# Exponentials of a chunk's last rows: a step on the PSUM read in place of a step on the SBUF write

## The chip, the cores and the metric

The kernel runs on one core of a Trainium2 chip. The metric is the device time of one execution in microseconds. Before the change it is 180.93 us, the median of 3 runs (180.81 to 181.0). A difference is read against runs of the kernel before on the same chip.

## What is computed

A gated linear attention over 4 batches, 8 heads, 768 steps and a head size of 48, and behind it one mixer block with weights over tokens (768 to 256 and back) and over channels (384 to 1536 and back). All matrices come in and go out as float32.

```python
f = 1.0 / (1.0 + np.exp(-f_logit))
for t in range(S):
    state = f[:, :, t, :, None] * state + np.einsum('bhd,bhe->bhde', k[:, :, t], v[:, :, t])
    y[:, :, t] = np.einsum('bhd,bhde->bhe', q[:, :, t], state)
x = np.ascontiguousarray(y.transpose(0, 2, 1, 3)).reshape(B, S, H * D)
xt = x.transpose(0, 2, 1)
u = x + (np.maximum(xt @ w_tok1, 0.0) @ w_tok2).transpose(0, 2, 1)
out = u + np.maximum(u @ w_ch1, 0.0) @ w_ch2
```

## The kernel before

**Tiling.** Each batch's 768 steps are cut into 6 chunks of 128, with the step on the partitions. Inside a chunk the recurrence is replaced by matmuls: the gates' logarithms are summed over the steps of the chunk by a matmul with a triangle of ones (L554, L555), and ScalarE takes from that bank in PSUM the exponential with both signs (`G` and `Gi`, L565 and L567). VectorE multiplies q by `G` and k by `Gi` in one operation (L586), TensorE turns the products (L603; for the last batch a DMA does that), the scores are made (L504), masked on VectorE into `AmT` (L640) and multiplied with v (L678). From chunk to chunk goes a `state`: L652 adds the chunk's own part, L654 multiplies by `glast`, the decay over the whole chunk, which is the exponential of the sum at the chunk's last step, and copies of it (`state_bd`, through the copy helper at L459 to L463) feed L671.

**Where the changed line stands.** `glast` must lie with the head's channel on the partitions: partition (par, d) and column hp, for head 2 hp + par and channel d. The sums have the step on the partitions. So for batches 1 to 3 and every chunk but the last (15 times) L574 takes the exponentials of the sums' last 32 rows (partitions 96 to 127, since an instruction begins at such a boundary here) into `ends`, and a small DMA (`across`, L580, on SyncE's queue) carries row 127 of `ends` to the 128 partitions of `glast`. `ends` is laid out as (par, d, hp) with room for 64 channels, so that row 127, read from front to back, gives each partition of `glast` its 4 floats side by side. The sums in PSUM are laid out as (hp, par, d). Batch 0 makes `glast` with matmuls of its own (L570). There are 4 buffers of `ends` and `glast`.

**The mixer.** L708 and L724 are the two token matmuls, L740 on VectorE adds the residual, L459 casts to `u_bf`, L765 turns it, L783 is the first channel matmul with its ReLU on ScalarE (L468) or VectorE (L470), L802 the second, with the residual on VectorE (L808) and the output's DMA (L812).

**What sets the order.** Every operation is entered with `add` into a plan, with the engines that may do it, a rank, a model of its cost and the bank of PSUM that it uses. The plan lays all operations out by this model, helped by a table of ranks and delays by operation number (`SHIFTS`), and the instructions are then issued in that order on each engine. The order is fixed when the kernel is built; each engine takes its instructions in turn and waits where one isn't ready. The model's cost of L574 is that of 384 elements from PSUM, `el = ("el", DM, True, 1)`, whatever the steps of its operands. The kernel uses 8 banks of PSUM; a bank comes free for the next matmul when its last reader is done, and L574 is one of the readers of the sums' bank.

Of the kernel before, what the change touches and what calls it, by code (L numbers as in the profile page):

```python
# [12 lines left out]
AF = mybir.ActivationFunctionType  # L13
# [103 lines left out]
class Plan:  # L117
# [11 lines left out]
    def add(self, engines, rank, fn, need=(), make=(), bank=None, kind=("fix", 100, 100), tail_of=None, room=1):  # L129


        engines = (engines,) if isinstance(engines, str) else engines
        op = Op(engines, rank, fn, need, make, bank, kind)
        for key in need:
            if key in self.maker:
                op.before.add(self.maker[key])
        for key in make:
            if key in self.maker:
                op.before.add(self.maker[key])
            op.before.update(self.users.get(key, ()))  # L140
        for key in need:
            self.users.setdefault(key, []).append(op)
        for key in make:
            self.maker[key], self.users[key] = op, []
        if bank is not None:
            key = bank
            if key in self.maker:
                op.before.add(self.maker[key])
            if engines == (PE,):
                self.maker[key] = op  # L150
        if kind[0] == "load":
            line = self.loads[engines[0]]
            if line:
                op.behind = line[-1]
            line.append(op)
        op.room = room
        if tail_of is not None:
            while tail_of is not None:
                tail_of.before |= op.before - {tail_of}
                tail_of.tail = tail_of.tail or op  # L160
                tail_of = next((x for x in self.ops if x.tail is tail_of), None)
        self.ops.append(op)
        return op
# [137 lines left out]
def kernel(  # L301
# [13 lines left out]
    B, H, S, D = q.shape  # L315
# [11 lines left out]
    def st(shape, dtype, tag):  # L327
        return sb.tile(shape, dtype, tag=tag, name=tag)
# [26 lines left out]
    ends = [st([128, 2, 64, HP], FP32, f"ends{i}") for i in range(4)]  # L355
# [131 lines left out]
    def attention(b, cs, due):  # L487

        nb = b % NB
        heads = [sums_and_turns(b, c, due(b, c) - (3.0 if b >= TURNED else 0.0)) for c in cs]  # L490
        p_d, live = Bank(), [c for c in cs if c < NCH - 1]
        need = [("qkT", c % 4, p) for c in cs for p in range(2)]
# [37 lines left out]
    def sums_and_turns(b, c, r):  # L530
        i, i4, nb, g4 = c % 2, c % 4, b % NB, (b * NCH + c) % 4
# [29 lines left out]
        def sview():  # L561
            return banks[p_s.at][:, 0:DM].rearrange("t (h d) -> t h d", d=D)
# [6 lines left out]
        if not last and b < 1:  # L569
            add(ACT, r + 1.0, lambda: nc.scalar.activation(  # L570
                glast[g4], banks[p_s.at][:, DM:DM + HP], AF.Exp, bias=0.0, scale=-1.0),
                make=[("glast", g4)], bank=p_s, kind=("el", 4, True, 1))
        elif not last:
            add(ACT, r, lambda: nc.scalar.activation(  # L574
                ends[g4][96:128, :, 0:D].rearrange("t par d hp -> t hp par d"),
                sview()[96:128].rearrange("t (hp par) d -> t hp par d", par=2), AF.Exp, bias=0.0, scale=-1.0),
                make=[("ends", g4)], bank=p_s, kind=el)

            def across():
                nc.sync.dma_start(out=glast[g4], in_=ends[g4][127:128].rearrange("o par d hp -> o (par d) hp"))  # L580

            add(SP, r, across, need=[("ends", g4)], make=[("glast", g4)],
                kind=("fix", 600, (5200, 5200, 3400)[b - 1], 300))
# [299 lines left out]
```

## Time and profile before

| | |
|---|---|
| median of 3 runs | 180.93 us |
| the profiled execution | 180.95 us, of which the span of its instructions is 179.1 us |
| granted TensorE clock | 1.00 |
| busy: TensorE, VectorE, ScalarE, GpSimd | 166.3, 128.1, 125.8, 100.7 us |
| L574, all 15 | 12.7 us of ScalarE, first at 39.3, last at 129.2 us |
| L580, the DMA behind it | 15 times 2 KB, 4.3 us from issue to landing (median) |

PE is TensorE (PEld its weight loads), DVE is VectorE, ACT is ScalarE, POOL is GpSimd and SP is SyncE. A row of a group gives line, engine, operation, what is written from what is read, shapes and count, then the group's busy time, the mean of one in ns, and the idle time before its instructions with what ended it. A row of the timeline gives start and duration in us, engine, line, operation and count (instructions of one kind in a row are merged), and in brackets the idle time before it and the instruction that ended it. A row of the windows gives the stretch, its length and the busy time of each engine in it, the granted clock, and the share and rate of the DMA.

### The profile page before, as it was taken

To read this page: it belongs to the slowest core of one execution; us is meant where nothing else is said; L and a number is where in the kernel's file an instruction comes from. 1 tells how busy PE (TensorE), PEld (TensorE's weight loads), DVE (VectorE), ACT (ScalarE), POOL (GpSimd) and SP (SyncE) were. 2 spreads that over 40 slices of the span, in tenths; PEclk is the share of its full clock that TensorE was granted. 3 is DMA by queue.
4 is the path that set the end of the run, shared out by engine and by line. 5 is a ranking of instruction groups with operands and counts; after the bars stand their busy time and mean duration, and the time that the engine had idled before them with its cause. 6 is when DMAs were issued, how large, how long until landed. Compare 5 with 4: busy or idle time off the path is not lost.

```text
span 179.1 us, 4283 instructions
## 1 busy us (share of the span) xinstructions
PE 166.3 (93%) x1649; PEld 104.8 (59%) x1653; DVE 128.1 (72%) x286; ACT 125.8 (70%) x273; POOL 100.7 (56%) x136
## 2 busy tenths in 40 slices
PE   6888898899998999799899999999999999999991
PEld 2445565556665665465566656676666666656660
DVE  6469886996878999887949987699674666501331
ACT  4678894699798786999899689976844432695000
POOL 7999569696599969977992996521102211000000
PEclk9999999999999999999999999999999999999999
DMA  7999999999999999999997999944812011200132
GB/s 105 127 165 157 148 149 182 211 142 203 183 167 152 213 247 91 199 91 89 113 161 40 89 201 137 189 91 108 93 31 89 3 44 47 90 0 0 73 117 77
DMA packets 97796, 21.54 MB, mean 120 GB/s; under 512 B 90512, under 2 KB 96912, under 8 KB 97776
## 3 DMA queue, kind: packets, MB, share of 16 engines
q0 software_dynamic: 79440, 13.77, 96.1%
q1 hardware_dynamic: 18336, 7.51, 19.0%
q8 instruction: 13, 0.21, 0.6%
q14 instruction: 7, 0.06, 0.1%
HBM read 25.17 MB, written 4.72 MB: 167 GB/s over the span
## 4 chain that ended last, share of the span: by engine, by line
PE 46%; ACT 11%; DVE 3%; issue 1%
PE ps L802 19%; PE ps L783 15%; ACT ends L574 3%; PE ps L724 2%; PE ps L708 2%; ACT zT L468 2%; PE ps L765 1%; ACT u_bf L459 1%; ACT GG L567 1%; PE ps L504 1%; PE ps L678 1%; PE ps L671 1%; PE ps L603 1%; ACT f_sb L479 1%; ACT state_bd L459 1%
## 5 line engine op out<-in xcount | busy, mean ns | idle before, releaser
L783 PE MATMUL ps<-uT,w_ch 128*128 128x384 bf16 x288 | 51.9, 326 | 1.2 <-ACT zT L468 0.7
L802 PE MATMUL ps<-w_ch,zT 128*128 128x384 bf16 (+2 forms) x300 | 52.4, 320 | 0.0
L468 ACT ACTIVATE zT<-ps 128x384 bf16<-128x384 f32 x70 | 33.2, 491 | 12.2 <-PE ps L783 9.9
L783 PEld LDWEIGHTS <-w_ch 128*128 128x128 bf16 x288 | 27.2, 98 | 18.1 <-issue 1.6
L802 PEld LDWEIGHTS <-zT 128*128 128x128 bf16 x300 | 27.7, 98 | 16.6
L640 DVE TENSOR_TENSOR AmT<-ps,tri_bf 128x512 bf16<-128x512 f32 x46 | 29.9, 683 | 3.3 <-PE ps L504 3.1
L401 POOL DMA_DIRECT2D v_sb<-in_v_dram x24 | 22.4, 931 | 4.7 <-DMA w_ch<-in_moe_w_ch_dram 4.7
L808 DVE TENSOR_TENSOR x_nat<-x_nat,ps 128x384 f32<-128x384 f32 (+2 forms) x25 | 13.3, 535 | 15.4 <-PE ps L802 15.3
L401 POOL DMA_DIRECT2D qk_sb<-in_k_dram x24 | 22.7, 944 | 0.8 <-POOLq L867 0.8
L401 POOL DMA_DIRECT2D qk_sb<-in_q_dram x24 | 22.6, 944 | 0.0
L470 DVE TENSOR_SCALAR zT<-ps 128x384 bf16<-128x384 f32 x26 | 13.8, 551 | 8.7 <-PE ps L783 8.7
L586 DVE TENSOR_TENSOR qk<-qk_sb,GG 128x768 bf16<-128x768 bf16 (+1 forms) x30 | 14.9, 501 | 6.0 <-ACT GG L567 2.6
L463 POOL CAST state_bd<-state 48x192 bf16<-48x192 f32 x13 | 4.4, 342 | 21.8 <-DVE state L654 11.4
L401 POOL DMA_DIRECT2D f_sb<-in_f_logit_dram x18 | 16.5, 943 | 0.2
L479 ACT ACTIVATE f_sb<-f_sb 128x384 f32<-128x384 f32 x24 | 12.4, 517 | 4.9 <-DMA f_sb<-in_f_logit_dram 4.7
L603 PE MATMUL ps<-ident,qk 128*128 128x128 bf16 x144 | 11.4, 220 | 1.9 <-DVE qk L586 1.8
L849 PE MATMUL ps<-steady 128*128 128x512 bf16 x37 | 11.6, 433 | 1.6 <-DVE steady L433 1.5
L574 ACT ACTIVATE ends<-ps 32x384 f32<-32x384 f32 x15 | 12.7, 861 | 0.3
L459 ACT ACTIVATE state_bd<-state 48x192 bf16<-48x192 f32 x27 | 9.7, 360 | 4.2 <-DVE state L654 3.5
L565 ACT ACTIVATE GG<-ps 128x384 bf16<-128x384 f32 x24 | 11.6, 488 | 1.4 <-PE ps L555 1.1
L603 PEld LDWEIGHTS <-qk 128*128 128x128 bf16 x144 | 8.8, 98 | 5.8 <-DVE qk L586 4.2
L567 ACT ACTIVATE GG<-ps 128x384 bf16<-128x384 f32 x24 | 11.3, 493 | 0.5 <-PE ps L555 0.3
(75 smaller groups left out, 249.2 us busy)
## 6 DMA issues: line engine op xcount, KB each, us to landing
out_dram<-x_nat SPq DMA_DIRECT2D x23, 192.0 KB, 3.0
f_sb<-in_f_logit_dram POOLq DMA_DIRECT2D x18, 192.0 KB, 5.4
qk_sb<-in_k_dram POOLq DMA_DIRECT2D x24, 96.0 KB, 5.3
qk_sb<-in_q_dram POOLq DMA_DIRECT2D x24, 96.0 KB, 5.5
v_sb<-in_v_dram POOLq DMA_DIRECT2D x24, 96.0 KB, 5.3
f_sb<-in_f_logit_dram SPq DMA_DIRECT2D x6, 192.0 KB, 4.1
w_ch<-in_moe_w_ch_dram POOLq DMA_DIRECT2D x2, 576.0 KB, 8.6
w_ch<-in_moe_w_ch_dram POOLq DMA_DIRECT2D x1, 1152.0 KB, 10.2
```

Source lines behind the costliest of these rows:

```text
L401: lambda eng=eng, into=into, of=of: eng.dma_start(out=into, in_=of),
L459: nc.scalar.activation(out_, in_, AF.Copy, bias=0.0, scale=1.0)
L468: nc.scalar.activation(out_, in_, AF.Relu, bias=0.0, scale=1.0)
L470: nc.vector.tensor_scalar(out_, in_, 0.0, None, ALU.max)
L479: add(ACT, r, lambda: nc.scalar.activation(fb, fb, AF.Exp, bias=0.0, scale=-1.0), make=[key], kind=el)
L574: add(ACT, r, lambda: nc.scalar.activation(ends[g4][96:128, :, 0:D].rearrange("t par d hp -> t hp par d"), sview()[96:128].rearrange("t (h ...
L586: add(DVE, r, lambda n=n: nc.vector.tensor_tensor(qk[i4][:, n, :, 0:D], qk_sb[nb][:, n, :, c, :], GG[i][:, n], ALU.mult), need=[(x, nb, c) ...
L603: nc.tensor.transpose(to[:, o + hp, :], blk(src)[:, hp, :], ident)
L640: add(DVE, r, lambda half=half, made=made: nc.vector.tensor_tensor(half, made(), tb4, ALU.mult), need=["tri_bf"], make=[("AmT", i, p)], ba ...
L783: nc.tensor.matmul(banks[pm.at][:, 0:384], lhsT=w[:, kt, c0:c0 + 128], rhs=uT[:, th, :, kt, :], start=(kt == 0), stop=(kt == 2))
L802: nc.tensor.matmul(banks[pm.at][:, 0:n1 - n0], lhsT=zT[:, kt, tt * 128:(tt + 1) * 128], rhs=w_ch2[:, kt, n0:n1], start=(kt == 0), stop=(kt ...
L808: add(DVE, rank("ch2", tt), lambda un=un, pm=pm, n=n1 - n0: nc.vector.tensor_tensor(un, un, banks[pm.at][:, 0:n], ALU.add), make=[("x_nat" ...
```

## The change

The two operands of L574 are given in another order of their dimensions. Before, the elements are taken in the order (hp, par, d): the read of PSUM is 384 floats in a row, and the write to SBUF places consecutive floats 4 floats (16 bytes) apart, in 8 runs of 48. After, they are taken in the order (par, d, hp): the read takes 4 floats that lie 96 floats (384 bytes) apart, then steps by one channel, and the write is 192 floats in a row, twice. The same values land at the same addresses. The plan's entries, their number, their ranks and the model's costs are the same, so the order of all instructions is too.

```diff
         elif not last:
             add(ACT, r, lambda: nc.scalar.activation(
-                ends[g4][96:128, :, 0:D].rearrange("t par d hp -> t hp par d"),
-                sview()[96:128].rearrange("t (hp par) d -> t hp par d", par=2), AF.Exp, bias=0.0, scale=-1.0),
+                ends[g4][96:128, :, 0:D],
+                sview()[96:128].rearrange("t (hp par) d -> t par d hp", par=2), AF.Exp, bias=0.0, scale=-1.0),
                 make=[("ends", g4)], bank=p_s, kind=el)
```

## The prediction

> **What bounds the kernel now.** I read the busy shares first, then the chain that ended last, then the windows, and only then single instructions.
>
> ```profile
> span 179.1 us, 4283 instructions
> PE 166.3 (93%) x1649; PEld 104.8 (59%) x1653; DVE 128.1 (72%) x286; ACT 125.8 (70%) x273; POOL 100.7 (56%) x136
> PE 46%; ACT 11%; DVE 3%; issue 1%
> PE ps L802 19%; PE ps L783 15%; ACT ends L574 3%; PE ps L724 2%; PE ps L708 2%; ACT zT L468 2%; PE ps L765 1%; ACT u_bf L459 1%; ACT GG L567 1%; PE ps L504 1%; PE ps L678 1%; PE ps L671 1%; PE ps L603 1%; ACT f_sb L479 1%; ACT state_bd L459 1%
> ```
>
> TensorE is busy for 93% of the span, so over all there are only 12.8 us to be had from anything that isn't a matmul. But ScalarE holds 11% of the last chain, and the changed line, L574, is its largest item there. Where TensorE has gaps is a matter of stages:
>
> ```profile
> 54.00:60.00 6.00, 5.31 (x74) 3.53 (x72) 5.45 (x11) 4.80 (x11) 6.00 (x8) 1.00 1.93 199
> 66.00:72.00 6.00, 5.51 (x58) 3.35 (x55) 5.69 (x12) 4.39 (x13) 4.70 (x6) 1.00 1.20 111
> 72.00:78.00 6.00, 4.80 (x47) 3.13 (x46) 5.53 (x14) 5.90 (x13) 4.93 (x6) 1.00 1.97 184
> 84.00:90.00 6.00, 5.07 (x40) 3.09 (x40) 5.55 (x13) 5.19 (x12) 6.00 (x7) 1.00 1.24 92
> 90.00:96.00 6.00, 5.74 (x75) 3.75 (x73) 3.62 (x7) 5.72 (x13) 3.64 (x5) 1.00 1.70 142
> 102.00:108.00 6.00, 5.70 (x81) 3.72 (x74) 5.46 (x12) 5.44 (x13) 6.00 (x8) 1.00 1.86 175
> 108.00:163.00 55.00, 55.00 (x495) 35.11 (x492) 35.33 (x76) 36.04 (x74) 10.84 (x21) 1.00 0.48 74
> ```
>
> The columns are the stretch, its length, then the busy time of PE, PEld, DVE, ACT and POOL. TensorE stands for 0.69, 0.49, 1.20, 0.93, 0.26 and 0.30 us in the first six, together 3.87 us, and ScalarE is nearly full in 72 to 78 and 90 to 96. From 108 to 163 TensorE is busy without a gap: nothing that ScalarE gains there is worth anything, but an earlier arrival at 108 is kept to the end.
>
> **What the changed instruction costs.** It writes 384 exponentials per row. Today it reads PSUM in a row and writes every fourth float (16 bytes apart); after the change it reads with a step of 96 floats (384 bytes), in runs of 4, and writes in runs of 192. The ScalarE groups, each with its own shape:
>
> ```profile
> L574 ACT ACTIVATE ends<-ps 32x384 f32<-32x384 f32 x15 | 12.7, 861 | 0.3
> L565 ACT ACTIVATE GG<-ps 128x384 bf16<-128x384 f32 x24 | 11.6, 488 | 1.4 <-PE ps L555 1.1
> L459 ACT ACTIVATE x_nat<-ps 128x384 f32<-128x384 f32 x15 | 7.3, 490 | 3.0 <-PE ps L678 1.8 <-DVE x_bf L461 1.1
> L468 ACT ACTIVATE h1T<-ps 128x192 bf16<-128x192 f32 x2 | 0.7, 330 | 0.6 <-PE ps L708 0.6
> ```
>
> L565 computes the same exponential of the same bank with as many elements per row, and L459 writes as many floats: 488 and 490 ns. The 192-wide row at 330 ns gives the slope: 160 ns for 192 elements, 0.83 ns each, on a base of 170 ns. The step on the write thus costs 861 - 490 = 371 ns, or about 1 ns more per element. The change takes that step away, which is certain, and puts one on the read, which no row here shows: no instruction of this trace reads PSUM with a step. Bounds: at the low end the read costs nothing extra and the instruction takes 0.49 us; it can't well be shorter, since at 384 elements of 0.83 ns both forms of write take that. At the high end the read pays twice the excess of the stepped write, 490 + 2 x 371 = 1.23 us (each element from a word of its own, and 96 short runs in place of 8 long ones). Even is 0.861 us. I take 0.49 us: the nearest rows on the read's side are L565 and L459, which are fed from PSUM at 0.83 ns an element, and the one slow row is explained by its write to SBUF, which goes.
>
> The Trainium skill (Advanced Engine Details and Errata, section Memory Cachelines) gives SBUF lines of 16 bytes, of which at least two accesses should hit the same line; the 861 against 490 ns of one float per 16 bytes agrees. The same section gives PSUM lines of 8 bytes and wants every two consecutive elements side by side, though it says so of matmuls. Carried over to ScalarE it speaks against the change: each float would come from another line, the instruction would stay near 0.86 us, and the time near 180.9; by the unpenalised read it is the sum below.
>
> **What 371 ns is worth, place by place.** No instruction moves; the DMA at L580 behind each L574 issues as before, only earlier. I follow the 15 instructions to TensorE. The wait in brackets is what stood before the instruction.
>
> ```profile
> 51.69 0.86 ACT L574 ACTIVATE ends<-ps 32x384 f32<-32x384 f32 x1
> 52.57 0.49 ACT L459 ACTIVATE x_nat<-ps 128x384 f32<-128x384 f32 x1
> 53.10 0.56 DVE L461 CAST x_bf<-ps 128x384 bf16<-128x384 f32 x1 [0.75 <-ACT x_nat L459]
> 54.63 0.55 DVE L586 TENSOR_TENSOR qk<-qk_sb,GG 128x768 bf16<-128x768 bf16 x1
> 55.24 0.62 PE L603 MATMUL ps<-ident,qk 128*128 128x128 bf16 x8 [0.69 <-DVE qk L586]
> ...
> 71.13 0.87 ACT L567 ACTIVATE GG<-ps 128x384 bf16<-128x384 f32 x2
> 72.96 1.56 ACT L574 ACTIVATE ends<-ps 32x384 f32<-32x384 f32 x2
> 72.98 2.87 DVE L740 TENSOR_TENSOR x_nat<-x_nat,ps 128x384 f32<-128x384 f32 x6
> 74.54 2.59 ACT L459 ACTIVATE u_bf<-x_nat 128x384 bf16<-128x384 f32 x6
> 75.12 0.23 PE L765 MATMUL ps<-ident,u_bf 128*128 128x128 bf16 x1 [0.29 <-ACT u_bf L459]
> 75.53 0.23 PE L765 MATMUL ps<-ident,u_bf 128*128 128x128 bf16 x1 [0.18 <-ACT u_bf L459]
> 75.95 0.56 PE L765 MATMUL ps<-ident,u_bf 128*128 128x128 bf16 x7 [0.18 <-ACT u_bf L459]
> 77.19 0.45 PE L765 MATMUL ps<-ident,u_bf 128*128 128x128 bf16 x5 [0.17 <-ACT u_bf L459]
> ```
>
> First place: L574 at 51.69 delays a copy, that delays VectorE by 0.75 us, and VectorE the transposes that TensorE waited 0.69 us for. 0.37 us fits into both waits: **0.37**. Second: two in a row hold up six casts, on which TensorE waits four times, 0.82 us together. Two PSUM exponentials back to back take 0.87 us (the GG pair at 71.13), so 1.56 becomes 0.87: **0.69**. VectorE ends the last of its six sums at 75.85; the last cast, now begun about 76.6, would begin about 75.9, so the sums just let it.
>
> ```profile
> 81.08 0.85 ACT L574 ACTIVATE ends<-ps 32x384 f32<-32x384 f32 x1
> 83.58 0.56 DVE L461 COPY x_nat<-ps 128x384 f32<-128x384 f32 x1 [0.97 <-ACT x_bf L459]
> 84.19 1.14 PE L783 MATMUL ps<-uT,w_ch 128*128 128x384 bf16 x6 [0.43 <-DVE x_nat L461]
> 86.82 0.85 ACT L574 ACTIVATE ends<-ps 32x384 f32<-32x384 f32 x1
> 88.23 2.11 PE L783 MATMUL ps<-uT,w_ch 128*128 128x384 bf16 x12 [0.74 <-ACT zT L468]
> 90.79 0.85 ACT L574 ACTIVATE ends<-ps 32x384 f32<-32x384 f32 x1
> 92.57 0.56 DVE L586 TENSOR_TENSOR qk<-qk_sb,GG 128x768 bf16<-128x768 bf16 x1 [1.63 <-ACT GG L567]
> 93.18 0.62 PE L603 MATMUL ps<-ident,qk 128*128 128x128 bf16 x8 [0.26 <-DVE qk L586]
> 102.76 0.87 ACT L574 ACTIVATE ends<-ps 32x384 f32<-32x384 f32 x1
> 105.21 0.33 PE L671 MATMUL ps<-state_bd,qkT 128*128 128x96 bf16 x4 [0.30 <-ACT state_bd L459]
> ```
>
> Third: the one at 81.08 delays ScalarE's queue up to the copy that VectorE waits 0.97 us for, and TensorE then 0.43: **0.37**. Fourth, at 86.82: TensorE waits 0.74 for the ReLU behind it: **0.37**. Fifth, at 90.79: only 0.26 of wait are left: **0.26**. Sixth, at 102.76: **0.30**. These are in series, since after each TensorE runs on from its own queue, and 0.37 + 0.69 + 0.37 + 0.37 + 0.26 + 0.30 = 2.36 us. The other eight lie where TensorE didn't wait for ScalarE (36 to 48, 54 to 60, 108 to 130), and count nothing; their cover is the matmul queue, and without it they would bring 8 x 0.37 = 3.0 us more. What is late next at each of the capped places is TensorE itself.
>
> The profiled execution took 180.95 us for its span of 179.1, which is 0.02 us over the median of the runs, 180.93. 180.95 - 2.36 = **178.6 us**.
>
> **The rivals.** *The read costs what the write did* (the PSUM rule above, as a mechanism of this kernel: 384 separate accesses at about 1 ns extra). L574 stays at 0.86 us, the waits stay, 180.9 us. For it: the write shows that a step can double an instruction. Against it: L565 and L459 show nothing of what PSUM gives with a step, so nothing but the likeness supports it. *Slower: the stepped read costs more than the stepped write.* Its place is the same queue; it decides from 0.861 us on. At 1.23 us the seven instructions on the chain are 0.37 us longer each, waits have no cap upward, 7 x 0.37 = 2.6: 183.5 us. For it: ScalarE has no room in 72 to 78 (5.90 of 6.00), and the read's inner runs shrink from 384 in a row to 4. Against it: a word per element would have to cost twice what SBUF's line does. *Shorter, but the gain is caught up.* Gains accumulate only if loads and VectorE come earlier too. GpSimd issues the loads and is full in 54 to 60 and 84 to 90; if the later half of the places (0.37 + 0.37 + 0.26 + 0.30 = 1.30) goes to such waits, 1.06 are left: 179.9. Against it: TensorE names no load among what it waited for in these stages.
>
> **How the numbers follow.** The forecast gets 0.54, the equal read 0.15 (180.9), the slower one 0.25 (183.5 at its far end), the caught-up gain 0.06 (179.9). Differences under 0.2% (0.36 us) can't be told from none with this kernel. Faster is the forecast and the caught-up gain, 0.60; same 0.15; slower 0.25. The forecast's own range is 178.0 to 179.9: downward two fifths of the 3.87 - 2.36 = 1.5 us of waits left in the windows (0.6), upward the caught-up gain. The whole range is 178.0 to 182.6: the upper end holds reads up to 0.861 + 1.65 / 7 = 1.10 us and leaves the dearer ones, about 0.14, outside, with about 0.05 below.
>
> **What would show it.** L574's mean in the changed profile decides first: about 0.49 us (ScalarE's busy time then falls by 15 x 0.37 = 5.6 us to about 120), 0.86, or over that. Then the waits of TensorE at L603, L765 and L783 in 54 to 95: the six above should shrink by their terms. If L574 is short and they stay, the chain that I followed was wrong; if they shrink and new waits stand between 108 and 163, the gain was given back. A mean above 0.87 us refutes the forecast outright.

## The result and the profile after

The changed kernel takes 178.47 us (median of 4 runs, 178.07 to 179.08) against 180.97 us for the kernel before (180.81 to 181.01): a ratio of 0.9866, 95% interval [0.9836, 0.9897], 2.5 us less. The profiled execution took 178.30 us for a span of 176.5 us.

The page of the changed kernel, its busy shares and its last chain:

```profile
span 176.5 us, 4283 instructions
PE 165.9 (94%) x1649; PEld 104.7 (59%) x1653; DVE 127.1 (72%) x286; ACT 120.3 (68%) x273; POOL 100.9 (57%) x136
PE 51%; ACT 5%; DVE 3%; issue 0%
```

ScalarE is busy for 5.5 us less and holds 5% of the chain in place of 11%; L574 is gone from the head of its items. The ScalarE groups of the changed kernel, by shape:

```profile
L565 ACT ACTIVATE GG<-ps 128x384 bf16<-128x384 f32 x24 | 11.6, 487 | 1.6 <-PE ps L555 1.4
L459 ACT ACTIVATE x_nat<-ps 128x384 f32<-128x384 f32 x15 | 7.3, 490 | 3.2 <-PE ps L678 1.8 <-DVE x_bf L461 1.1
L574 ACT ACTIVATE ends<-ps 32x384 f32<-32x384 f32 x15 | 7.1, 483 | 0.3
```

L574 takes 483 ns, as little as the exponentials and copies that read PSUM in a row. TensorE's stages, in the same stretches as before (stretch, length, busy time of PE, PEld, DVE, ACT, POOL):

```profile
54.00:60.00 6.00, 5.69 (x76) 3.80 (x75) 5.37 (x11) 4.33 (x10) 6.00 (x8) 1.00 1.91 203
66.00:72.00 6.00, 5.14 (x50) 3.08 (x49) 5.65 (x12) 4.37 (x12) 5.17 (x7) 1.00 1.24 114
72.00:78.00 6.00, 5.64 (x55) 3.88 (x55) 6.00 (x15) 5.90 (x14) 5.44 (x8) 1.00 2.13 181
84.00:90.00 6.00, 5.63 (x46) 3.46 (x42) 4.64 (x10) 5.14 (x13) 6.00 (x8) 1.00 1.72 117
90.00:96.00 6.00, 6.00 (x76) 3.93 (x74) 5.34 (x9) 5.68 (x14) 3.40 (x4) 1.00 1.22 118
102.00:108.00 6.00, 6.00 (x65) 3.77 (x62) 5.21 (x11) 5.74 (x14) 6.00 (x8) 1.00 1.99 167
```

The idle time of TensorE in them falls from 3.87 to 1.90 us. (In 66 to 72 the idle time rises, from 0.49 to 0.86, only because the matmuls that began at 72.44 behind a wait of 0.38 us now begin at 71.97.) The instructions of TensorE that answer to the prediction's six places, in the changed kernel's timeline, with the wait before them in brackets:

```profile
46.97 2.12 PE L802 MATMUL ps<-w_ch,zT 128*128 128x384 bf16 x12
...
54.77 0.62 PE L603 MATMUL ps<-ident,qk 128*128 128x128 bf16 x8 [0.31 <-DVE qk L586]
...
74.78 0.56 PE L765 MATMUL ps<-ident,u_bf 128*128 128x128 bf16 x7 [0.18 <-ACT u_bf L459]
...
76.02 0.45 PE L765 MATMUL ps<-ident,u_bf 128*128 128x128 bf16 x5 [0.17 <-ACT u_bf L459]
...
83.62 0.33 PE L671 MATMUL ps<-state_bd,qkT 128*128 128x96 bf16 x4
...
86.33 2.11 PE L783 MATMUL ps<-uT,w_ch 128*128 128x384 bf16 x12 [0.37 <-ACT zT L468]
...
90.91 0.62 PE L603 MATMUL ps<-ident,qk 128*128 128x128 bf16 x8
...
102.58 0.33 PE L671 MATMUL ps<-state_bd,qkT 128*128 128x96 bf16 x4
```

Set against the timeline of before, the same instructions come earlier by 0.08 (47.05 there), 0.47 (55.24), 1.17 (77.19), 1.54 (85.16), 1.90 (88.23), 2.27 (93.18) and 2.63 us (105.21). The steps of this ladder are what each place gave: 0.39, 0.70, 0.37, 0.36, 0.37 and 0.36 us, **2.55** together, after 0.08 us that lay in the start. Of the two rows of before that weren't shown yet, one opens the ladder and one closes the third step:

```profile
47.05 2.12 PE L802 MATMUL ps<-w_ch,zT 128*128 128x384 bf16 x12
...
85.16 0.33 PE L671 MATMUL ps<-state_bd,qkT 128*128 128x96 bf16 x4
```

Behind 105 us nothing is won or lost: the long run of 60 matmuls near the end begins at 154.05 us in the chain of before and at 151.42 in that of the changed kernel, again 2.63 us apart. First the piece of before:

```profile
154.05 9.75 PE ps L783 x60
```

and the piece of the changed kernel:

```profile
151.42 9.75 PE ps L783 x60
```

These two marks, the 12 matmuls near 47 us and the 60 near 154, serve as a ruler below: the stretch between them leaves the start out, which varies by almost 1 us from one execution to the next. Before it is 107.00 us, after 104.45. The changed kernel was traced three times, at 104.45, 104.45 and 104.48; every other kernel has one trace, and a difference of a tenth on the ruler says little.

### The profile page after: what moved, and what is told of

The parts are those of the page before. It is cut to its first block, busy times and chain, and to the rows that moved or that the text cites. A ratio compares the mean times of both kernels' runs of the same rounds, so it can differ in the third digit from the quotient of the medians.

```text
span 176.5 us, 4283 instructions
## 1 busy us (share of the span) xinstructions
PE 165.9 (94%) x1649; PEld 104.7 (59%) x1653; DVE 127.1 (72%) x286; ACT 120.3 (68%) x273; POOL 100.9 (57%) x136
## 4 chain that ended last, share of the span: by engine, by line
PE 51%; ACT 5%; DVE 3%; issue 0%
PE ps L802 20%; PE ps L783 17%; PE ps L708 2%; PE ps L724 2%; PE ps L504 2%; PE ps L765 1%; ACT u_bf L459 1%; DVE AmT L640 1%; PE ps L678 1%; PE ps L603 1%; PE ps L520 1%; PE ps L671 1%; PE ps L554 1%; DVE x_nat L808 1%; PE ps L555 1%; ACT ends L574 1%
## 5 line engine op out<-in xcount | busy, mean ns | idle before, releaser
L586 DVE TENSOR_TENSOR qk<-qk_sb,GG 128x768 bf16<-128x768 bf16 (+1 forms) x30 | 14.2, 479 | 4.7 <-ACT GG L565 2.2
L740 DVE TENSOR_TENSOR x_nat<-x_nat,ps 128x384 f32<-128x384 f32 x21 | 10.5, 546 | 0.8 <-PE ps L724 0.7
```

Of the source, the lines that this page charges most:

```text
L586: add(DVE, r, lambda n=n: nc.vector.tensor_tensor(qk[i4][:, n, :, 0:D], qk_sb[nb][:, n, :, c, :], GG[i][:, n], ALU.mult), need=[(x, nb, c) ...
```

## The experiments

### What a step costs, by itself

```diff
     for op in plan.best(idle, 6500.0, 25500.0):
         op.fn()
+    line = L[0].rearrange("t c h d -> t (c h d)")
+    bank = banks[0][:, 0:384]
+    act = lambda to, of: nc.scalar.activation(to, of, AF.Exp, bias=0.0, scale=-1.0)
...
+    for _ in range(4): act(line[96:128, 0:384], bank[96:128])
...
+    for _ in range(4): act(line[96:128, 0:384].rearrange("t (s a) -> t s a", s=96), bank[96:128].rearrange("t (a s) -> t s a", s=96))
...
```

> The changed kernel with a bench behind its work: 384 floats per row, four times each, read from PSUM or SBUF and written to SBUF with steps of 1, 2, 3, 4, 8 and 96 floats on one side or on both, on 32 or 128 partitions, as exponentials on ScalarE and as copies on VectorE. The whole is some 60 us longer; only the means of the bench's rows are of interest. Theory (a stepped read of PSUM is free, a write is dear from 16 bytes on): 0.48 us for every read from PSUM with a step and a write in a row; 0.48 for writes with a step of 2 floats, 0.86 for 4, 8 and 96; both stepped 0.86. Rival (the 4 floats a line rule counts lines changed per element, so 12 bytes already cost): 3 floats in between, some 0.6 to 0.7. Rival for the read (only the changed instruction's own pattern is free): a read with a step of 2 or 4 floats over 0.6. The skill's 8-byte lines of PSUM would make every stepped read 0.8 or more.

The bench of this kernel, grouped by shape in one stretch for each form (four of each; mean ns behind the busy time). On ScalarE, 32 partitions, PSUM read with steps of 1, 2, 4 and 96 floats and SBUF written in a row:

```profile
L856 ACT ACTIVATE L<-ps 32x384 f32<-32x384 f32 x4 | 1.9, 483 | 4.4 <-DVE x_nat L808 4.3
...
L856 ACT ACTIVATE L<-ps 32x384 f32<-32x384 f32 x4 | 1.9, 482 | 0.1
...
L856 ACT ACTIVATE L<-ps 32x384 f32<-32x384 f32 x4 | 1.9, 483 | 0.1
...
L856 ACT ACTIVATE L<-ps 32x384 f32<-32x384 f32 x4 | 1.9, 482 | 0.1
```

No step shows on the read. Next, PSUM read in a row and SBUF written with steps of 2, 3, 4, 8 and 96 floats:

```profile
L856 ACT ACTIVATE L<-ps 32x384 f32<-32x384 f32 x4 | 2.0, 499 | 0.1
...
L856 ACT ACTIVATE L<-ps 32x384 f32<-32x384 f32 x4 | 2.7, 668 | 0.1
...
L856 ACT ACTIVATE L<-ps 32x384 f32<-32x384 f32 x4 | 3.3, 835 | 0.1
...
L856 ACT ACTIVATE L<-ps 32x384 f32<-32x384 f32 x4 | 3.4, 848 | 0.1
...
L856 ACT ACTIVATE L<-ps 32x384 f32<-32x384 f32 x4 | 3.2, 812 | 0.1
```

Two floats (8 bytes) cost next to nothing, three (12 bytes) half of the penalty, four (16 bytes) all of it, and more than that no more. The 668 ns at 12 bytes are what the rival said (0.6 to 0.7); the theory had the write dear only from 16 bytes on. The line rule that the Trainium skill gives for SBUF (Advanced Engine Details and Errata, section Memory Cachelines) fits each of these (of every four floats that lie 12 bytes apart, two share a line); its 8-byte lines of PSUM don't show on ScalarE's reads. That was the rule that spoke against the change. With steps of 4 or 96 on both sides the means are 835 and 812 ns, the same as with the step on the write alone, and 128 partitions give 490 and 842 ns in place of 483 and 835.

A source in SBUF pays as a destination there does; steps of 1 and 4 floats on the read, the write in a row:

```profile
L856 ACT ACTIVATE L<-L 32x384 f32<-32x384 f32 x4 | 2.1, 518 | 0.1
...
L856 ACT ACTIVATE L<-L 32x384 f32<-32x384 f32 x4 | 3.5, 875 | 0.1
```

VectorE does as ScalarE does: a copy from PSUM takes 557 ns with a read's step of 96 and 829 ns with a write's step of 4:

```profile
L857 DVE COPY L<-ps 128x384 f32<-128x384 f32 x4 | 2.2, 557 | 0.1
...
L857 DVE COPY L<-ps 128x384 f32<-128x384 f32 x4 | 3.3, 829 | 0.1
```

### A step on both sides in the kernel

```diff
-                ends[g4][96:128, :, 0:D],
-                sview()[96:128].rearrange("t (hp par) d -> t par d hp", par=2), AF.Exp, bias=0.0, scale=-1.0),
+                ends[g4][96:128, :, 0:D].rearrange("t par d hp -> t hp d par"),
+                sview()[96:128].rearrange("t (hp par) d -> t hp d par", par=2), AF.Exp, bias=0.0, scale=-1.0),
```

> All 15 instructions with a step on both sides: elements in the order (hp, d, par), so that PSUM is read 48 floats and SBUF written 256 floats apart. Same values at the same addresses. Theory (the read's step is free, the write's costs 0.35 us): L574 0.81 to 0.85 us and the time of before, a ratio of 0.998 to 1.000. Rival (both steps cost, and add up): 1.2 us and 183 us or more.

The ratio is 1.0005 [0.9978, 1.0032]: the whole gain is lost, though PSUM is read with a step in this kernel too. L574 takes 895 ns, 34 more than before and more than the 0.81 to 0.85 us expected, which no run explains, but far from the rival's 1.2 us:

```profile
L574 ACT ACTIVATE ends<-ps 32x384 f32<-32x384 f32 x15 | 13.2, 895 | 0.3
```

On the ruler it is 107.64 us, 0.64 over before. Of that 0.24 are there by the matmuls near 105 us, and TensorE's waits at the first five of the six places are longer by 0.03 to 0.09 us each. Another 0.33 is a wait for a DMA that no other run shows:

```profile
118.54 0.62 PE L504 MATMUL ps<-qkT 48*128 48x128 bf16 x16 [0.33 <-DMA qkT<-qk]
```

So it is the write's step that the kernel pays for, and taking it away is what the change does.

### Seven of the fifteen, and the other eight

```diff
-                ends[g4][96:128, :, 0:D],
-                sview()[96:128].rearrange("t (hp par) d -> t par d hp", par=2), AF.Exp, bias=0.0, scale=-1.0),
+                *((ends[g4][96:128, :, 0:D], sview()[96:128].rearrange("t (hp par) d -> t par d hp", par=2))
+                  if (b, c) in ((1, 3), (2, 0), (2, 1), (2, 2), (2, 3), (2, 4), (3, 0)) else
+                  (ends[g4][96:128, :, 0:D].rearrange("t par d hp -> t hp par d"),
+                   sview()[96:128].rearrange("t (hp par) d -> t hp par d", par=2))), AF.Exp, bias=0.0, scale=-1.0),
```

> The new operand order only at the seven instructions that were followed to TensorE (51.7, 73.0 twice, 81.1, 86.8, 90.8 and 102.8 us in the trace of before); the other eight as before. Theory (ScalarE's queue delays TensorE at six places, nowhere else): all of the gain, 178.5 us, within 0.3 of the changed kernel; L574's mean (7 x 0.483 + 8 x 0.857) / 15 = 0.68 us. Rival (each of the 15 brings its share, 7/15 of 2.5 us): 179.8 us.

> The new order only at the other eight instructions (39.3, 43.0, 54.2, 59.8, 108.7, 113.2, 117.1, 129.2 us). Theory: nothing, 180.9 us, within 0.3 of before, though ScalarE is busy for 8 x 0.37 = 3.0 us less. Rival (each brings its share, 8/15 of 2.5): 179.6 us.

The selection was wrong in one place: batch 3, chunk 0 is the instruction at 108.7 us, and the one at 102.8 is chunk 1. So the seven held six that count and one that doesn't, and the eight held one that counts. That can be read: the seven gave 0.9875 [0.9832, 0.9917] and 104.83 us on the ruler, 0.38 short of the changed kernel, with the wait at 103 us still there,

```profile
103.35 0.33 PE L673 MATMUL ps<-state_bd,qkT 128*128 128x96 bf16 x4 [0.30 <-ACT state_bd L459]
```

and the eight gave 0.9985 [0.9964, 1.0007] and 106.66 us, 0.34 less than before. One instruction at the right place is worth its 0.36 us; the one at 108.7, which the seven held in its stead, is worth nothing, as the eight of the next pair show. With `(3, 1)` in place of `(3, 0)`:

> As the first run, with the selection mended: there the last of the seven was the instruction at 108.7 us, not the one at 102.8. Now the new order stands at 51.7, 73.0 twice, 81.1, 86.8, 90.8 and 102.8 us of the trace of before. Theory: all of the gain, a ratio to before of 0.987 as for the changed kernel, and 0.002 below that of the first run's selection; TensorE no longer waits at L673 near 103 us. Rival (each of the 15 brings its share): 7/15 of the gain, a ratio of 0.994, and the same as with the first selection.

> The other eight, 39.3, 43.0, 54.2, 59.8, 108.7, 113.2, 117.1 and 129.2 us. Theory: a ratio of 1.000, with TensorE's waits near 55, 75, 84, 88, 93 and 105 us as before. Rival: 8/15 of the gain, 0.993.

> The changed kernel once more, beside its two halves on the same chip: a ratio of 0.987, equal to the seven's within 0.002.

| the new order at | ratio to before | ruler, us |
|---|---|---|
| none (before) | 1 | 107.00 |
| the eight | 1.0006 [0.9986, 1.0027] | 107.03 |
| the seven | 0.9871 [0.9851, 0.9891] | 104.46 |
| all fifteen, on the same chip | 0.9850 [0.9828, 0.9873] | 104.45 |

The eight make ScalarE's work 2.8 us less (123.0 us busy against 125.8) and shorten nothing; the seven bring all of it, and TensorE no longer waits near 103 us. The times alone are too coarse for the finer expectations: the two selections of seven differ by 0.0004 where 0.002 was expected, and the seven and all fifteen by 0.0021, with wide intervals; the ruler shows the 0.37 us between the two selections (104.83 and 104.46) and none between the seven and the fifteen. The rival by which each instruction brings a share is out: its 0.993 and 0.994 lie outside both intervals.

### Two alone

The same edit with the selection `(b, c) in ((2, 3), (3, 0))`.

> The new order only at the two instructions whose worth was capped by TensorE's shown waits (90.8 and 102.8 us). With the caps as predicted, 0.26 + 0.30 = 0.56 us: 180.4 us. If the shown waits are short by what the modelled ends of matmuls hide, the whole 0.37 twice, 0.74: 180.2 us, and TensorE's instructions behind 105 us come 0.7 us earlier than in the trace of before, those behind 94 us 0.37 earlier.

Here too the second was the instruction at 108.7 us, so the run speaks for the one at 90.8 alone. The ratio is 0.9967 [0.9939, 0.9995], an interval too wide to tell 0.26 us from 0.37. This kernel's matmuls that wait for the ReLU near 88 us, from its timeline:

```profile
88.60 0.65 PE L785 MATMUL ps<-uT,w_ch 128*128 128x384 bf16 x3 [0.74 <-ACT zT L468]
```

and its run of 60, from its chain:

```profile
154.05 9.75 PE ps L785 x60
```

From the one to the other it is 65.45 us, and 65.82 before (88.23 to 154.05): 0.37 us for an instruction whose cap had been put at 0.26. On the whole ruler this kernel stands at 106.75 us, only 0.25 less than before: in this execution the transposes near 55 us, far ahead of the changed instruction, waited 0.80 us in place of 0.69. The place itself shows the 0.37 without any ruler, in this kernel:

```profile
92.64 0.65 PE L785 MATMUL ps<-uT,w_ch 128*128 128x384 bf16 x3
93.18 0.62 PE L605 MATMUL ps<-ident,qk 128*128 128x128 bf16 x8
```

The transposes begin 0.54 us behind the three matmuls, where it was 0.91 before (92.27 to 93.18). The cap was read off the wait that the profile shows, and that wait is too short. In the timeline of before the matmuls in front of it are

```profile
92.27 0.65 PE L783 MATMUL ps<-uT,w_ch 128*128 128x384 bf16 x3
```

shown as ending at 92.92, 0.26 before the transposes at 93.18. But 60 of them in a row take 9.75 us in the chain, 0.163 each, so by this estimate the next could have begun at 92.27 + 3 x 0.163 = 92.76, and there was room for 0.42 us. In the kernel with all fifteen the three matmuls begin at 90.36 and the transposes at 90.91, 0.55 us behind them.

### No L574 at all

```diff
-        once(DVE, lambda i=i: nc.vector.memset(ends[i][96:128, :, D:64], 1.0), [("ends", i)], 200)
+        once(DVE, lambda i=i: nc.vector.memset(ends[i][96:128], 1.0), [("ends", i)], 200)
...
-            add(ACT, r, lambda: nc.scalar.activation(
-                ends[g4][96:128, :, 0:D],
-                sview()[96:128].rearrange("t (hp par) d -> t par d hp", par=2), AF.Exp, bias=0.0, scale=-1.0),
+            add(ACT, r, lambda: None,
                 make=[("ends", g4)], bank=p_s, kind=el)
```

> The changed kernel without the 15 exponentials of L574: ends holds ones, so the decay between chunks is left out in batches 1 to 3. It asks what is left in them. Theory (worth only what TensorE still waits for ScalarE: 0.31 near 55 us, 0.37 near 86 us, and part of 0.35 near 75 us, where VectorE's six sums are next): 0.7 to 1.0 us less than the changed kernel, a ratio to before of 0.982. Rival (ScalarE's queue sets these stages, each of the seven is worth its 0.48 us): 3 us less, 0.970.

The ratio is 0.9831 [0.9803, 0.9859], and the ruler 103.28 us, 1.17 less than the changed kernel's 104.45 and more than the 0.7 to 1.0 expected. The waits that went, 0.31 and 0.37 us and 0.02 of the 0.35 near 75, are 0.70 of it; the other 0.47 came beyond the waits that the profile shows, 0.22 of it ahead of the matmuls that the changed kernel has at 83.62, which show none. Some 7 us of ScalarE's work are taken away for this: most of the 483 ns that are left in each L574 is covered, and with this order of instructions no further saving in this line can bring more than 1.2 us.

### Moved back instead

```diff
...
-    for op in plan.best(idle, 6500.0, 25500.0):
+    line = plan.best(idle, 6500.0, 25500.0)
+    for key, n in [((1, 3), 1), ((2, 4), 2)]:
+        at = next(j for j, op in enumerate(line) if op.tag == key)
+        to = [j for j, op in enumerate(line) if j > at and op.engine == ACT][n - 1]
...
+    for op in line:
         op.fn()
```

> The changed kernel with two of the 15 moved back on ScalarE: the one at 51.6 us behind the copy that follows it, the one at 85.3 behind the two ReLUs that follow it, each with its DMA. Theory: the copy and the ReLUs come 0.48 us earlier, TensorE's waits of 0.31 near 55 us and 0.37 near 86 us go, 0.5 to 0.7 us less than the changed kernel, a ratio of 0.983. Rival (the work that is now pushed back is missed as much, or a bank held longer stops a matmul): no gain or a loss, 0.987 or above.

The ratio is 0.9842 [0.9810, 0.9873], and the ruler 104.17 us, only 0.28 less than the changed kernel where 0.5 to 0.7 were expected. Both waits went, but a new one came up further on, in the timeline of this kernel:

```profile
90.68 0.62 PE L604 MATMUL ps<-ident,qk 128*128 128x128 bf16 x8 [0.22 <-DVE qk L587]
```

It hangs on another of the 15, the one before `G` and `Gi` near 88.7 us. With `((2, 3), 2)` moved as well:

> The changed kernel with three of the 15 moved back on ScalarE: the two of the run before, and the one near 88.7 us behind the two exponentials (G and Gi) that follow it and that VectorE's product near 90 us waits for. Theory: the wait of 0.22 us that came up at L603 near 91 us goes as well, and 0.5 to 0.7 us less than the changed kernel beside it are left, 177.9 us. Rival (a new wait comes up again within some us): no difference to the changed kernel beyond 0.2 us.

> The changed kernel beside the one with three moved: 178.5 us, a ratio to before of 0.986.

178.19 us and 0.9819 [0.9792, 0.9845] against 178.64 us and 0.9855 [0.9831, 0.9878] for the changed kernel beside it. The intervals overlap, so by time alone it isn't settled, but the ruler gives 103.72 against 104.48 us, 0.76 less (0.5 to 0.7 were expected), and between 50 and 110 us TensorE waits only for the operands of the second token matmul and of the turns behind it. It has the shortest median of the kernels here that compute the whole.

## Why the prediction was right, point by point

- *The read's step costs nothing*: right, 483 ns where 0.49 us had been taken. The choice went by the nearest rows, and none of them reads with a step, so no row decided it, and that it came out is in part luck. The bench shows that it holds for steps of 2, 4 and 96 floats. The equal read (180.9 us) and the dearer one (183.5) are out with it.
- *The write's step costs 371 ns*: right, 861 - 483 = 378.
- *Six places, seven instructions*: right, shown by the seven and the eight. On the ladder the terms 0.37, 0.69, 0.37, 0.37 measured 0.39, 0.70, 0.37, 0.36.
- *The caps of 0.26 and 0.30 at the fifth and sixth place*: mis-sized; they measured 0.37 and 0.36, the whole saving. The prediction took the waits shown before the instructions as the room there was. At the fifth it was 0.42 by the estimate above, since a matmul's shown end lies behind the time at which the next can begin. At the sixth 0.29 came where the 0.30 were shown, and 0.07 at the L671 ahead of it, which shows no wait but began 0.23 us behind the matmul before it (103.82 and 104.05) and in the changed kernel begins 0.16 behind it (101.55 and 101.71). The prediction has TensorE itself late next at these two places; within a saving of this size it wasn't.
- *The sum*: 2.36 predicted, 2.55 on the ladder; the profiled execution fell by 180.95 - 178.30 = 2.65 and the medians by 2.50. Of the 0.10 us beyond the ladder, 0.08 lie in the start.
- *Nothing given back*: right as well; near 105 us and at the run of 60 matmuls the distance to before is the same 2.63 us. The caught-up gain had no part in it: TensorE shows no new wait for a load.
- *The other eight would bring 3.0 us more without their cover*: not tried; what the runs show is that under it they bring nothing.

## What to carry to other kernels

When a transposing copy leaves PSUM for SBUF, put the step on the PSUM side and write in a row: here 4 bytes written every 16 bytes or more cost 0.81 to 0.90 us for 384 floats, where steps of 2, 4 and 96 floats on the read cost 0.48. Price such a saving by the places where the bottleneck waits for that queue, not by its sum: 5.6 us on ScalarE were worth 2.55. And take the gaps that this profile shows before matmuls as lower bounds of the room there is: 0.26 us were shown where 0.37 were gained.

## What was not expected of the hardware

- The penalty of a stepped write is graded: 483, 499, 668 and 835 ns for steps of 4, 8, 12 and 16 bytes, and no more beyond (848 and 812 ns at 32 and 384 bytes). A stepped read of SBUF by ScalarE pays alike, 518 ns in a row against 875 at 16 bytes.
- VectorE reads PSUM with steps of 8, 16 and 384 bytes as fast as in a row (557 against 558 ns), and pays for a stepped write in SBUF (829 ns at 16 bytes).
- A stepped read of PSUM adds nothing to a stepped write: 4 floats on both sides took 835 ns, as on the write alone.
- The time from the first instruction to the marks near 47 us varies by 1 us between executions (46.95 to 47.92 us for the same matmuls, over all traces), while the stretch behind them agrees to 0.03 us in the three traces of the changed kernel. It isn't always so steady: in the run of the two alone a wait ahead of the change was 0.11 us longer. Differences of a few tenths were still seen far sooner between two marks in the trace than in the times.
